# Hash-routed experts behind a gated recurrence: row numbers carried in the sorted rows, tiles read in twos, weights cast by the DMA of GpSimd, eleven sorted groups, 54 chunks scanned by way of TensorE

## The chip, the cores and the metric

The kernel runs on one core of one Trainium2 chip. The metric is the device time of one execution in microseconds, the median of three. A profile is one further execution, taken with the hardware profiler, with a trace of every instruction and of every DMA packet.

## What is computed

The reference has two parts. The first is a gated recurrence over the sequence; the second sends each of its output rows through one of eight small networks, chosen by a hash of the token's id.

```
x, f_logit: [4, 5056, 256] f32;  lower_bound: [256];  token_ids: [20224];  w1: [8, 256, 1024];  w2: [8, 1024, 256]
f = lower_bound + (1 - lower_bound) * sigmoid(f_logit)
for t in range(5056):
    h = f[:, t] * h + (1 - f[:, t]) * x[:, t]
    y[:, t] = h
expert = token_ids * 2654435761 % 8
out[rows of e] = relu(y[rows of e] @ w1[e]) @ w2[e]
```

The multiplier leaves 1 modulo 8, so the expert is the low three bits of the id. Each expert gets 16 of 128 tokens on average.

## The kernel before

The 20224 tokens are cut into 158 chunks of 128 (32 positions of the four sequences), and these into 24 blocks (`TS`), most of them of eight chunks.

**Scan.** A block's `f_logit` and `x` are loaded with one row per token, but the scan instruction runs along the free axis, so features have to lie on partitions. In the first `KS = 7` blocks (46 chunks) TensorE transposes each chunk (L743), ScalarE and VectorE make the gate (L747 to L758), VectorE scans (L773), TensorE transposes back (L812) and ScalarE or VectorE evicts to `yT` (L826). In the other blocks VectorE transposes in 32 x 32 pieces, before and after (L926, L988), with its scan in L969. A block begins where the one before it ended, so scans follow one another.

**Sort.** Each token's place in `srt`, a buffer in DRAM with 21 tiles of 128 rows (`CAP`) for each of eight experts, is worked out from the ids by one-hot tables, scans and matmuls (`rank_*`). Chunks before the middle fill an expert's rows from below and chunks after it from above, and some tiles in between are zero-filled first (`fill`). GpSimd scatters `yT` to `srt` row by row, one indirect DMA per chunk (L676). For seven blocks the last four chunks go another way: a one-hot matrix (L1010) sorts 512 rows by expert in TensorE (L1017), the result is put to a scratch buffer, and eight plain DMAs of 104 rows from SyncE (`move`, L1052), with addresses read from registers (`regs`), move each expert's segment to its place. Scatters after such a block wait for its moves.

**Row numbers.** The output rows have to go back to their tokens. For each block `tb` builds one-hot matrices of rank and tile on VectorE (L1093 to L1104), `tpe` multiplies them on TensorE (L1110) and `tadd` adds the result to a table and makes `row_i` (L1117 to L1126).

**Experts.** A tile of 128 rows of one expert is read when all blocks that can reach it have landed (`win`, `last`). A transposing DMA from SyncE brings it as `xe` (L1158). TensorE makes 1024 hidden values by 16 matmuls of 128 columns (L1168), ScalarE or VectorE applies the relu (L1177, L1179) to `hT`, TensorE goes down with eight matmuls of 256 columns (L1186), the result is evicted for two tiles at a time (L1194, L1196) and GpSimd scatters 128 rows to the output (L1200), one indirect DMA per tile.

**Weights** come through the same two staging buffers as `f_logit` and `x`, in f32, by SyncE (L640, L644), and ScalarE or VectorE casts them to bf16 (L653, L655).

**Order.** Each engine works through its instructions in the order in which they are written. The order of all tasks is a list found beforehand by a search over estimated costs and priorities, which is written into the file as a compressed string (`ORDER`) that also says whether ScalarE or VectorE takes each task that either can do. The costs and priorities in the `add` calls are remains of that search and change nothing at run time. Buffers are short rings (`xe` 8, `hT` 3, PSUM `hp` 2 and `op` 4), and a task that takes a buffer waits for the one that used it before.

After all this a flag is read; only where a count was outside its bounds does a slow loop over all chunks run. With these inputs it is not entered.

Of the kernel before, what the change touches and what calls it, by code (L numbers as in the profile page):

```python
# [11 lines left out]
FP32 = mybir.dt.float32  # L12
# [8 lines left out]
E = 8  # L21
# [6 lines left out]
KS = 7  # L28
# [7 lines left out]
RANGES = [(0, 6), (6, GA), (GA, MID), (MID, NG)]  # L36
FILL = (9, 12)
FB = {GA: [9, 10, 11], MID: [13, 15, 17, 19]}
FS = [k for a in (GA, MID) for k in FB[a]]
GF = len(FS)  # L40
FA = ()
SEG = 104
XF = 3
OFF, TABD = 20.0, 25.0
W0, W1 = -70.0, 6.0
# [3 lines left out]
    "c-"  # L49
    "jrsgQ8_Q5CFiayEC?J+qP}nww06Q&U<6qwr$(CZCkrPQ5D9d;jAx<&ib(ttUnvTMzMj6u^4PH10z^8Glq?1;cTc`#A2~HEQJ}w5;J9nu#_ePi^+x"  # L50
    "=W8$*WY#Iy93}($Z=Ga&hfh}d8#b%4yc(aKuV-rjyGo7Vl6U`D9ku_zLSSquE5u3$kvQ;br+rnm><!mL}%qFu_EWJr>uCc9b8=GS?noMS{*=|;w5"
    "ZlM*u{9<eTWjXC?B)#H&knGgY=_Bg*0C&XI9tzlnxyQ4-^C8GgX}bG!LphgEQdL4j+k5QEW6Imv7=@;Yi91S^X3?9#s0B{tT{W*E|`1lE-"
    "T9}s+KH1tH3V%OFjv^Xr{6&DyQN661(anoAPEao5F50!7nq(ulZ-}zPau{u@@{JTfl0vimVQ+Z626%?4e1-"
    "DzTSr4?DpUvRdpj+rXZ)jg0YEtS)<PzAzOeH(%LRc7@erCm96aSY_6cRbv=@HyPm(tIvLztWd>tVqMrzb3;95#Ph%}_Qo_~Rn1#d0IIW0po5$Kma"
    "oAg@OLa5bT$o4HOLIvAq(VyH0C#J&Dycj@Sb%w4Owx>3;Cd%dCCexW0s3GVQpD5^M_S}LZQDbKjaK`XKhSGe%t3ZY0U>#7)n3~Qxe*<NW2V`f{(0"
    "7sHb_t%0ds;i&cg@svJ~@@}VlB$o#I4!lUuJPy-V2KBg+f;4yh`lY~d-v4W^Pc2E=I1i2s=Zv*LgvY-"
    "~^=5d3>JZX@J=i_;U{6PjDk0%e(^AthKpg_<9;`3s>9yEkZycEyF>O;YxI4{F9^2|Y&pe)a88bN8Eisyzxyc|!>%LmnXVO|lc^BO#B&=`tAXXwQ%"
    "1pS}^WaCYsCa)OO;w5-?-"
    "V|2wdwvx!3N7KjU(b8<D6Ax}9khbB(2iH)jd(uO4l46HL3e1v6Y>On4S%3I@Gj6A@|$9;6Yt0?K;57RbcHm$Jw!E4c|YDPc<76pw7fBI9&~{AydL"
    "iy^x-{W0B;fG<lUe@AH)Yi4&Dpu^OiwX-imh#R&vdX@`1b#^oG8?YcPvDJ~(L2&+<9^3NOM#yc<tphXk{EcRn;2&OIN;!*~Nep0DHQ`6WJ&&*kTM"  # L60
    "e^|{g@U{Gr4-Y2r`N1&WkT-`(d?FtVm-&cbWUwG;!w10RpeJ7#wB?KVD87MD2|n?w-"
    "0+RTR=zhF0*m?7U{i3B@8|o19{els1XcKEzKo|62l+tQ#((l3d>S9kuLU>x7hW5N!XchfSiY2h<_Gu~m;hV&bZ+6X5BP0<Jt)MQ!FRqqxWTsvhl3"
    "r#FgP9*U}O32;ApTj*cFW7xA<><Cm0Te%?y4w*b@{qkAf%a33uQjtC-"
    "1;1yA`i9tKPJbT|?`^CyDm+`w4)#h>~IK{!l=aqu_@!E9IrGvHn@9!9`7-Vr9j{ouL(6Z{RL*nfNuFfkJXco8gv%p#h|BBI(e{7tYJxSb4h;Z-"
    "1PU&tYr!^>bJEP>a-NRW0G#I-HNTG#=5Ai7uznZ!KECSItM9PA2M32|&Z5nm{~4q{j>NTAIr4#O%q#rwc<h-DMl(|i-O6jLCkZ6y-"
    "f(Qpp3i&3y1BG{cUU95(Lb_28)5p6pW+dd2~!Dg5b?_n=Qvb!L$%_Sn+oAA<qh9i(t?1NMyw=H6xKt8br?!s1h<x`6^VmGXTBK8EN6>UUbQP}3ON"
    "1>P~D$c_UQQ79VCn1?Q1`DBzZ7-^dx50jBD^5Xi+d=$-0ye3rCSI!xa2aNai!c=m+LE?}eF3-"
    "N3Y4~GY&kIvl8EYdJ0uq$_y_+FYT5&E6+ZHNP{?)^x8V-du=k;?K-"
    "S4Vg?IcVl(+ABDVtu@vK4Ixu?^n%3U;=51|MJnG!>`8*#}U`b`^)9v;7EjM1A`T=82i2i?{|~pn>RS8;Os8u6Pb7#Y2dQ4Mk&t*xmN9pVV;SZ5&L"
    "FA<@(Rh9=?@y!C_ZIQtbCzEi#IL5P82cE0!nLqt9C4c`0LKzK?F6=&g#A8bE+j>BwXd;@=>kBEdC1;)fP5N;QU>oCIJfXMhAjIAx=Vmg!<3wzszw"  # L70
    "yx+aPK!Ds0zQTkEFO-uOGIE}<0Dusnu&h4xman>i71!^SBw5O6ArL%AwEXMq?iIz;svqDrpI@{rL}9sKr7`L@e?xRc##u#+TG#@EVU)gL@_~p^%-"
    "!Log|XsGP_481WbVEMJoKJE{W8b3-e+YTyEFe+*lrq;0jwAOJF{nEH>J8mgGed9XHvrVzbDI(Xbv0SroJ4dYd1|h&=eiZxP>pNgOS<+C-"
    "QZ6Jj<@gS+fDJ4Kuoqr_CP*KW5P>@=aImIbgF7Q}tF6xPCA@~1D3`)xj18Y^HKtb&(qQ*4RZF$WgLE_lEe!m?NnE8-"
    "4Y39r~v=C=K%UfZkUosA%`iK^HEYvTz4vJU?C^|1j~!|V2lxMOeFx1ugK#GCe*xGPGtd*Y~gV&B-u)?q|h9h+fu?2k{yecK8TiWYcW^v2fs-sX`V"
    "v8ZW-"
    "4{amtiq8bf5B9n3gl(~m>5RkhrR|1?#7BF}zOa4pfgOp5#djOoMRMJ70QSWm*ijmsf_ddw9Ebr%ku~v=ePwIlC!1Twa{aI|dh9F*VQlwTM3r%50o"
    "erGV=tVKA&lmtyBYXHByzt*JNzkPxKa3948}ixD~`svvL}wiotVn~5f;CR;W!l&yYZOXC6SBqs|dp(I1SUv&teQFbu)1l4#hMwo=fKb`Ytk^3&#a"
    "G0Sn3muCVMR*I`VTUw#p@a5~P$g&5yW#0-wfIhfEDlF8j79D)DTBwT_iToLzA%$Dh06<5YB#f7q%<e`-"
    "A0CtnBaT#WG%W(}Bm+P^d+<<ejs4L;h%bs#AR+HOMgid1%S6yz$l5QjJ!m6&TEbEToWSocRv6rmjcHl}}f!8pz+>M*Cf-"
    "B{+$vW;J=8zBZ5O$Xm_TXMTif6FCtmv}KvzS$~&@rs*>dDgX9L|+B-"  # L80
    "C?ZcYPl>jlYEK|TxE9)Yr6~B+YNS&+;wc|F5(STp)GhE8@ul~)a8_y(7W5%Lq5Vj?j~Nw)^eD<gD3DY4tGP`GyH%d*H_-"
    "f=Ll*uwv=yhp8SoHTFHKLAMVEpAyilKEndMk@*~cX?c_Urf)PV8slWSy_i%uFfdgGs`h<}nOh!_t@Fg~tgIrtr2Y=#dXWU{LS%o{I_qag*#n0GWe"
    "!(RYLQQ1g#!5vP8sn@RCx0QqKh&f{Cvm(3dVtX=a%hBGB$qnpMmk3Kae_mNKoebbdW{ijuZu(p=oQAIB-BiP!}hX+oG-"
    "s(YMSI?({d?@Q$pJ6F3C|Y8>Oc!@~TWkQ79Kh30;=kWm1YkaVRn^b35b;nTBS`sG+zN4bsv|myEW#=`t~`ay#7tx!Pr*eQt^@NEzw6%uZ`v8A?t?"
    "DILY9{c@e#AWymql!Fes!!9>XmNVr|xn8bud1#|cL76BgMGqZvg=mw@OSj~0S(u8^9k<z4r+id|;?Zt*Lr#^~<SzHdWv1fv#FeEZt|FD7a<s+Wca"
    "7+-t4-zUnbfKV?QzZMxqRxT$x3ua-jna-dwEKxqB_);9=M0DBt3F9sWQ!wDe0?=5h|=|QI)W_j?`)S!hLWZDP|}uHKwz&F4dzit_PJ;&8Z1BrH}5"
    "L%TEO;3$>%~t~4E!=Vc4(L`P+N>O-I0OIM%H$-"
    "xv={cxk`mn%g*sWWw;mJ|yjsxXS6`chSjq8__eVbT06*NY6r^e1F=Us4UB<FX&6^VO&e^`;nVDE)NF{cCqo26RFGcHz{JrczfLL9u*m>Q6;f2LIW"
    "`_HleNAI~?S0W^^;#R(0gHq?z`hvJ6f`#Drhb*GeSG$mAyMp6Qm!VjW9auTKYOnJ(v#?S)VM45alUsR2yxPCG%r_6pD&85{eol^TOehPI}xqLh*q"
    "h^p&GsA{ci008knxy8_xUdo`kuR;%_(e33_R<PkOe<*{CGlmwR8!O%66y?XrnR(+mQYo{g|^dQSzN87w7$IJYAYS23cinuAIj>xtHge?YU-"  # L90
    "2vYQCJ$t!nsv)J^ROtFC6#`ml;VkIJj|(=0kfCn%r)Coj`Zs^n|>+P<f%><`d&T1MH_1bRfx{bAZgC#i=zMfufPYUUG!>iR2mk8-"
    "FZRLh^E({wfLJl&xBzJ<!E`l>I~OI7jXsh;0J4SYY}&@ZKzw3}M`w{)M5(nczvdaDaGRTWg%Xb&~^H|a4wpkvg?5AX>?x2UzhO@-"
    "7Cnx$URacbqWtJgH!_xE*t6F*3`@y<unZ|EUCp^J2v!u(V6{v9bjP+g*VDqJm5gFVwBb%%!d1%9ULq&ljvlnCBaB%L_)fi|kRI-&ka-"
    ")N}cthT7(D!Vp*lj^K~(RW&?rm1I?B*gV^`WQCCi*V49bz6nuUDQ?;_@tp>e*6FJ{s~*`r>itNijJ=1{ZC1JJ<2D8xju!SuVREp)noill|Z*s9aM"
    "XjNXOJOR7#y#@A8?o^&@>+ojjCJr_wLzGmZAK!ava>Ki1FjN%TKTr?cp#{y7!WCG|m7R_pM;lvOYD6V-"
    "B`LyuE6bbg&$?^XMKHl1F_);m;AolEagg>_>cK^F*5stf82x|FV>i|9i>j^3t9>vDR6I^fs%eZIav>?7(Fq1<}6U+s(PBmSr#uUhGhy1Y)NSNbx#"
    "ovx~r>mj;=_PUrZu2=YKx~8tB8|byZq3)_z`O`j=uC9;!COVHk<6G;VdVnsWD~6x&jdX3j&NtPkd>ehtkJIh-"
    "N#9I&2;ZQ(>9%^3&a2P*IyxnE*Xva!-BI__J#=q9Q1{WDbn4J~HB^V|LHeAktn2CK;WPCxJy@rKkY1sOhqurpw9$3-T-{kO(c^WhP#4`dJZ-"
    "3@9;qkmKyTI)!o&2G@b!A49;MTTX6e~_s-CBp>S=m@cz@kbkJjm7nVzFp>IHg(UZ|~J74Gydy<Bh6tMzo9A+%Ai(PQ=2@ELlO-lrGq-"
    "FlneulMLhdW=30zE`i++x0<xD14pXsdwlj`mp{F4ZxtQ"  # L100
# [54 lines left out]
def kernel(  # L155
# [19 lines left out]
    WMAX = 8 * max(window(k)[1] - window(k)[0] + 1 for k in range(NB))  # L175
# [10 lines left out]
    srt = dram.tile([E * CAP, D], BF16, name="srt")  # L186
    scr = [dram.tile([4 * P + SEG, D], BF16, name=f"scr{i}") for i in range(3)]
    i32a = consts.tile([P, NT], I32, name="i32a")
    iota_lo = consts.tile([P, P], BF16, name="iota_lo")
    iota_hi = consts.tile([P, NT], BF16, name="iota_hi")  # L190
# [8 lines left out]
    Tab = consts.tile([P, 2, NT], FP32, name="Tab")  # L199
# [17 lines left out]
    ids7 = rp.tile([P, GA], I32, name="ids7")  # L217
    tok = rp.tile([P, NH, 32], I64, name="tok")
    tlow = rp.tile([P, NH * 32], I32, name="tlow")
# [13 lines left out]
    nmax = rp.tile([1, 2], FP32, name="nmax")  # L233
    handt = rp.tile([P, 8, 4], FP32, name="handt")
    row_id = rp.tile([P, NG], I32, name="row_id")
    row_t = rp.tile([P, NG], I32, name="row_t")
    lowt = rp.tile([P, NG], FP32, name="lowt")
    hight = rp.tile([P, NG], FP32, name="hight")
    eb_all = rp.tile([P, NG], BF16, name="eb_all")
    v1 = rp.tile([P, NG], BF16, name="v1")  # L240
    v2 = rp.tile([P, NG], BF16, name="v2")
    lo_h = rp.tile([P, NG], BF16, name="lo_h")
    hi_h = rp.tile([P, NG], BF16, name="hi_h")
# [12 lines left out]
    pl.pool("xe", 8)  # L256
    pl.pool("hT", 3)
    pl.pool("ob", 4)
    pl.pool("tb", 1)
# [6 lines left out]
    def init_pool():  # L266
        make_identity(nc, idf[:])
        nc.gpsimd.iota(i32a[:], pattern=[[1, NT]], base=0, channel_multiplier=0)
        make_upper_triangular(nc, up1[:], diag=False)

    def init_pool1():
# [5 lines left out]
        nc.gpsimd.memset(m8[:, :, 0:1], 0.0)  # L277

    def init_pool2():
        nc.gpsimd.memset(Tab[:], 0.0)  # L280
        nc.gpsimd.iota(
            oneh.rearrange("p c s -> p (c s)").bitcast(I32)[:, 512:1024].rearrange("p (j q) -> p j q", j=4),
            pattern=[[1, 4], [4, P]], base=0, channel_multiplier=0,
# [30 lines left out]
    def init_dve2():  # L314
        nc.vector.tensor_copy(iota8[:], i32a[:, :E])
        nc.vector.tensor_scalar(up1[:], up1[:], -1.0, None, op0=ALU.add)
        nc.vector.tensor_copy(idn[:], idf[:])
# [1012 lines left out]
```

## Time and profile before

| | us |
|---|---|
| time, median of three (lowest, highest) | 662.44 (650.76, 664.62) |
| the profiled execution | 499.46 |
| its span, first to last instruction | 497.7 |
| busy in it: TensorE, VectorE, ScalarE, GpSimd | 389.5, 391.3, 328.9, 320.9 |
| last matmul ends, last scatter starts | 485.3, 487.7 |
| mean granted TensorE clock | 0.906 of full speed |

The profiled execution is a quarter shorter than the timed ones; the profile doesn't show why. "Busy" counts an engine's instructions but not the issue of DMAs, which is what SyncE does (in the trace "SPq"). The share of the DMA engines is packets' time over that of 16 engines, and can pass 1.0 where packets overlap. "Idle before" and the waits name the last thing that an instruction waited for.

### The profile page before, as it was taken

To read this page: it belongs to the slowest core of one execution; us is meant where nothing else is said; L and a number is where in the kernel's file an instruction comes from. 1 tells how busy PE (TensorE), PEld (TensorE's weight loads), DVE (VectorE), ACT (ScalarE), POOL (GpSimd) and SP (SyncE) were. 2 spreads that over 40 slices of the span, in tenths; PEclk is the share of its full clock that TensorE was granted. 3 is DMA by queue.
4 is the path that set the end of the run, shared out by engine and by line. 5 is a ranking of instruction groups with operands and counts; after the bars stand their busy time and mean duration, and the time that the engine had idled before them with its cause. 6 is when DMAs were issued, how large, how long until landed. Compare 5 with 4: busy or idle time off the path is not lost.

```text
span 497.7 us, 12978 instructions
## 1 busy us (share of the span) xinstructions
PE 389.5 (78%) x4690; PEld 350.0 (70%) x4690; DVE 391.3 (79%) x916; ACT 328.9 (66%) x475; POOL 320.9 (64%) x385
## 2 busy tenths in 40 slices
PE   3655557885686997866997889799869978899990
PEld 2544446774586887756896779689859868899980
DVE  2799746899999899949898969898897896854430
ACT  2479445788787888656997769687757564565430
POOL 8066162457775767737777577776657776777772
PEclk9756588998798999979999899999989989999996
DMA  8999999999799989897999799699747773454521
GB/s 212 375 369 379 296 298 346 307 311 244 189 229 207 218 210 238 211 211 184 193 223 216 184 195 231 128 205 213 216 139 179 208 165 102 142 144 125 149 98 45
DMA packets 116035, 106.21 MB, mean 213 GB/s; under 512 B 59953, under 2 KB 99869, under 8 KB 115967
## 3 DMA queue, kind: packets, MB, share of 16 engines
q1 hardware_dynamic: 101743, 76.04, 60.5%
q0 software_dynamic: 12352, 29.28, 23.3%
q8 instruction: 38, 0.62, 0.6%
q10 hardware_dynamic: 1872, 0.02, 0.2%
q14 instruction: 30, 0.25, 0.2%
HBM read 61.47 MB, written 37.09 MB: 198 GB/s over the span
## 4 chain that ended last, share of the span: by engine, by line
PE 38%; DMA 17%; DVE 6%; ACT 5%; issue 4%; POOL 2%; SPq 2%; POOLq 0%; DVEq 0%; ACTq 0%
PE hp L1168 19%; PE op L1186 16%; DMA xe<-srt 14%; ACT hT L1177 3%; PE so L1017 2%; POOL out_dram L1200 2%; DVE y L969 2%; DMA f_t<-in_f_logit_dram 1%; SPq L1158 1%; DVE xT L952 1%; DVE sT L926 1%; DMA srt<-yT,pos_i 1%; ACT sT L940 1%; DMA x_t<-in_x_dram 1%; DVE xT L926 1%
## 5 line engine op out<-in xcount | busy, mean ns | idle before, releaser
L1200 POOL DMA_INDIRECT out_dram<-ob,row_i x168 | 172.8, 1028 | 75.9 <-issue 43.6
L1168 PE MATMUL hp<-xe,w 128*128 128x128 bf16 x2688 | 181.1, 226 | 50.7 <-DMA xe<-srt 40.4
L1177 ACT ACTIVATE hT<-hp 128x1024 bf16<-128x1024 f32 x152 | 153.7, 1023 | 85.7 <-PE hp L1168 67.4
L1168 PEld LDWEIGHTS <-w 128*128 128x128 bf16 x2688 | 167.8, 101 | 60.2 <-DMA xe<-srt 32.9
L676 POOL DMA_INDIRECT srt<-yT,pos_i x130 | 136.7, 1052 | 90.5 <-issue 33.8
L1186 PE MATMUL op<-w,hT 128*128 128x256 bf16 x1344 | 177.8, 284 | 9.4 <-ACT hT L1177 5.5
L1186 PEld LDWEIGHTS <-hT 128*128 128x128 bf16 x1344 | 131.4, 102 | 29.6 <-ACT hT L1177 7.7
L969 DVE TENSOR_TENSOR_SCAN y<-sT,y,xT 128x256 bf16<-128x256 f32 (+2 forms) x128 | 78.4, 645 | 0.2
L940 ACT ACTIVATE sT<-sT,lb_c,c_c 128x256 f32<-128x256 f32 (+2 forms) x109 | 57.9, 566 | 6.8 <-DVE sT L926 6.7
L1194 ACT COPY ob<-op 128x512 f32<-128x512 f32 x68 | 39.1, 585 | 17.7 <-PE op L1186 15.5
L926 DVE STREAM_TRANSPOSE xT<-x_t 128x512 f32<-128x512 f32 (+1 forms) x64 | 38.6, 619 | 13.7 <-DMA x_t<-in_x_dram 11.8
L952 DVE SCALAR_TENSOR_TENSOR xT<-sT,xT 128x512 f32<-128x512 f32 x56 | 37.2, 675 | 15.4 <-ACT sT L940 15.1
L1179 DVE TENSOR_SCALAR hT<-hp 128x1024 bf16<-128x1024 f32 x16 | 19.5, 1221 | 28.7 <-PE hp L1168 24.6
L926 DVE STREAM_TRANSPOSE sT<-f_t 128x512 f32<-128x512 f32 (+1 forms) x64 | 38.0, 613 | 0.1
L899 ACT ACTIVATE f_t<-f_t 128x1024 f32<-128x1024 f32 (+1 forms) x29 | 29.6, 1027 | 6.5 <-DMA f_t<-in_f_logit_dram 4.9
L773 DVE TENSOR_TENSOR_SCAN y<-sT,y,xT 128x256 bf16<-128x256 f32 (+1 forms) x48 | 31.4, 691 | 0.3
L1093 DVE TENSOR_TENSOR A<-iota_lo,lo_h 128x512 bf16<-128x512 bf16 (+1 forms) x41 | 26.8, 653 | 0.9 <-PE tp L1110 0.9
L812 PE MATMUL yp<-idn,y 128*128 128x128 bf16 x88 | 12.6, 266 | 17.3 <-DVE y L773 10.5
L743 PE MATMUL tf<-idf,f_t 128*128 128x128 f32 x92 | 17.7, 339 | 9.6 <-DMA f_t<-in_f_logit_dram 7.0
L988 DVE STREAM_TRANSPOSE yT<-y 128x256 f32<-128x256 f32 (+2 forms) x68 | 22.8, 363 | 0.0
L812 PEld LDWEIGHTS <-y 128*128 128x128 bf16 x88 | 7.6, 115 | 21.0 <-DVE y L773 15.8
L752 ACT ACTIVATE sT<-sT,lb_col,c_col 128x256 f32<-128x256 f32 x39 | 21.7, 596 | 0.2
(142 smaller groups left out, 314.2 us busy)
## 6 DMA issues: line engine op xcount, KB each, us to landing
f_t<-in_f_logit_dram SPq DMA_DIRECT2D x50, 256.0 KB
x_t<-in_x_dram SPq DMA_DIRECT2D x50, 256.0 KB
f_t<-in_moe_w_dram SPq DMA_DIRECT2D x8, 1024.0 KB
x_t<-in_moe_w_dram SPq DMA_DIRECT2D x8, 1024.0 KB
f_t<-in_f_logit_dram SPq DMA_DIRECT2D x10, 512.0 KB
x_t<-in_x_dram SPq DMA_DIRECT2D x10, 512.0 KB
srt<-scr SPq DMA_DIRECT2D x56, 52.0 KB
xe<-srt SPq DMA_TRANSPOSE x168
```

The costliest lines, as they stand in the source:

```text
L676: bi = nc.gpsimd.indirect_dma_start(out=srt[:], out_offset=bass.IndirectOffsetOnAxis(ap=pos_i[:, G0[k] + m:G0[k] + m + 1], axis=0), in_=T[ ...
L773: nc.vector.tensor_tensor_scan(yv[:, h, b, :tt], T["sT", un][:, h, c], T["vT", un][:, h, c], init, op0=ALU.mult, op1=ALU.subtract,)
L899: nc.scalar.activation(v, v, AF.Sigmoid)
L926: nc.vector.transpose(o, i_)
L940: nc.scalar.activation(v, v, AF.Identity, scale=c_c[:, c:c + 1], bias=lb_c[:, c:c + 1])
L952: nc.vector.scalar_tensor_tensor(x_.rearrange("p s c l -> p (s c l)"), f_.rearrange("p s c l -> p (s c l)"), 1.0, x_.rearrange("p s c l -> ...
L969: nc.vector.tensor_tensor_scan(yv(T["y", k])[:, cp, :L, s], T["sT", k, u][:, s, n, :], T["xT", k, u][:, s, n, :], init, op0=ALU.mult, op1= ...
L1168: nc.tensor.matmul(hp[:, f, :], lhsT=w1_sb[e][:, h, f * P:(f + 1) * P], rhs=xe[:, h, :], start=(h == 0), stop=(h == 1),)
L1177: nc.scalar.activation(hT[:], T["hp", j, e][:], AF.Relu)
L1186: nc.tensor.matmul(op[:, h, :], lhsT=T["hT", j, e][:, f, :], rhs=w2_sb[e][:, f, :], start=(f == 0), stop=(f == FF - 1),)
L1194: nc.scalar.copy(ob[:], T["op", n // 2][:])
L1200: bi = nc.gpsimd.indirect_dma_start(out=out, out_offset=bass.IndirectOffsetOnAxis(ap=row_i[:, c:c + 1], axis=0), in_=T["ob", n // 2][:, h, ...
```

## The change

It is one bundle of edits that hang together, with an order of its own (another `ORDER` string).

- **Row-number columns.** A row of `srt`, of the scratch buffers and of `yT` grows from 256 to 288 bf16 values (512 to 576 bytes). The added 32 columns repeat the token's row number as two values (`vv`), copied in once for each block (`id_cols`). When the tiles of column `j` are complete, SyncE reads four bytes of each of their 8 x 128 rows (`ids_in`), and two small VectorE operations make `row_i`. The table and its one-hot matrices go.
- **Tiles in twos.** For eight pairs of neighbouring tiles (`DUO`) both are read by one transposing DMA of 256 rows, and the up matmuls take 256 columns, four of the eight hidden slices at a time. Five tiles of each expert are still read singly, and these are paired across two experts for the eviction. `xe` has six buffers of twice the size, `hT` four.
- **GpSimd weight casts.** GpSimd loads each weight straight to bf16, with the cast in the DMA (`SW = range(8)`), instead of SyncE with casts on ScalarE and VectorE.
- **Eleven sorted groups** in place of seven: two before the middle, and all nine blocks of eight chunks after it. Three of them (`FA`) have their moves issued by ScalarE. Row numbers are sorted with the rows (`sort_ids`).
- **KS = 9:** two more blocks of 128 positions each sequence, eight chunks, are scanned by way of TensorE. Loads of these blocks from the fifth on are two per block, not four.
- The zero fill covers five tiles of each expert instead of three, and the flag also tests that the counts reach the filled region and that a segment isn't too short.

Its core:

```
-KS = 7
+KS = 9
-FB = {GA: [9, 10, 11], MID: [13, 15, 17, 19]}
+RA = 46
+FB = {RA: [9, 10], MID: list(range(12, 21))}
-FILL = (9, 12)
+FILL = [(8, 11), (11, 13)]
+RW = 288
-FA = ()
+FA = (2, 5, 8)
+DUO = [(1, 2), (3, 4), (5, 6), (7, 8), (12, 13), (14, 15), (16, 17), (18, 19)]
+XE, HT = 6, 4
+SW = range(8)
...
-    srt = dram.tile([E * CAP, D], BF16, name="srt")
+    srt = dram.tile([E * CAP, RW], BF16, name="srt")
...
+                    if v:
+                        nc.gpsimd.dma_start(w1_sb[e][:], moe_w1[e].rearrange("(s h k) f -> k s h f", s=2, h=2))
+                    else:
+                        nc.gpsimd.dma_start(w2_sb[e][:], moe_w2[e].rearrange("(q p) d -> p q d", p=P))
...
+    def id_cols(eng, k):
+        o = T["yT", k][:, :NGS[k], D:].rearrange("p m (r s) -> p m r s", s=2)
+        i_ = vv[:, G0[k]:G0[k] + NGS[k], None, :].to_broadcast((P, NGS[k], (RW - D) // 2, 2))
...
-        def tb(c0, c1, k=k, jlo=jlo, W=W):
-            nc.vector.tensor_tensor(
-                A[:, c0:c1, :], iota_lo[:, None, :].to_broadcast((P, n, P)),
-                lo_h[:, gs, None].to_broadcast((P, n, P)), op=ALU.is_equal,
-            )
...
-        def tpe(k=k, W=W, ng=ng):
-        def tadd(k=k, jlo=jlo, W=W):
+        def ids_in(j=j):
+            bi = nc.sync.dma_start(
+                row_v[:, j, :, :], srt.rearrange("(e c) d -> c e d", e=E)[j * P:(j + 1) * P, :, D:D + 2]
+            )
+        def ids_row(j=j):
+            nc.vector.scalar_tensor_tensor(
+                pi[:], row_v[:, j, :, 1], 256.0, row_v[:, j, :, 0], op0=ALU.mult, op1=ALU.add
+            )
+            nc.vector.tensor_scalar(row_i[:, E * j:E * j + E], pi[:], -1.0, None, op0=ALU.add)
...
-            bi = nc.sync.dma_start_transpose(xe[:], srt[r0:r0 + P, :])
+            bi = nc.sync.dma_start_transpose(xe[:, :, :w], srt[r0:r0 + w, :D])
...
-            for f in range(FF):
+            for n, f in enumerate(fs):
                 for h in range(2):
                     nc.tensor.matmul(
-                        hp[:, f, :], lhsT=w1_sb[e][:, h, f * P:(f + 1) * P], rhs=xe[:, h, :],
+                        hp[:, n * w:(n + 1) * w], lhsT=w1_sb[e][:, h, f * P:(f + 1) * P], rhs=rhs()[:, h, :],
```

## The prediction

> **What bounds the kernel now.** I read the engine table and the slices first, then stages, then waits, then the queue of SyncE.
>
> ```profile
> span 497.7 us, 12978 instructions
> ...
> PE 389.5 (78%) x4690; PEld 350.0 (70%) x4690; DVE 391.3 (79%) x916; ACT 328.9 (66%) x475; POOL 320.9 (64%) x385
> ...
> DMA  8999999999799989897999799699747773454521
> ```
>
> No engine is full, but three are near 80% or idle only at the ends. DMA is at nine tenths or more for most of the first two thirds. Three stages separate what an average mixes:
>
> ```profile
> core 0: us, PE busy (x) PEld busy (x) DVE busy (x) ACT busy (x) POOL busy (x), PEclk, DMA share, GB/s
> 25.00:125.00 100.00, 65.91 (x675) 56.50 (x675) 82.59 (x191) 69.88 (x106) 51.59 (x49) 0.77 1.06 318
> 125.00:375.00 250.00, 208.62 (x2591) 188.75 (x2592) 222.26 (x505) 189.72 (x275) 173.03 (x166) 0.94 0.92 202
> 375.00:488.00 113.00, 102.93 (x1357) 94.72 (x1354) 73.69 (x175) 60.28 (x80) 84.18 (x84) 0.98 0.55 145
> ```
>
> Columns: stage, its length, busy time and (instructions) of each engine, granted clock, DMA share. TensorE idles 34 us in the first stage (DMA over 1.0, low clock), 41 us in the second (VectorE at 89%), 10 us in the third. With 13 us of the first 25 and 10 us after 488 this is all of its 108 us idle (497.7 - 389.5). In the third stage GpSimd is full although it reads 74%: its indirect DMAs follow each other every 1.28 us, 0.97 busy and 0.30 of issue.
>
> ```profile
> 392.28 0.97 POOL L1200 DMA_INDIRECT out_dram<-ob,row_i  x1 [0.31 <-issue]
> 393.55 1.01 POOL L1200 DMA_INDIRECT out_dram<-ob,row_i  x1 [0.30 <-issue]
> 394.88 0.97 POOL L1200 DMA_INDIRECT out_dram<-ob,row_i  x1 [0.31 <-issue]
> ```
>
> The engine that no busy row shows is SyncE, whose queue issues in order. In the middle of the kernel:
>
> ```profile
> 320.93 2.46 SPq L1158 DMA_TRANSPOSE xe<-srt  x2
> 323.43 1.08 SPq L876 DMA_DIRECT2D f_t<-in_f_logit_dram  x2
> 324.62 1.17 SPq L1158 DMA_TRANSPOSE xe<-srt  x1
> ```
>
> There is no gap: a transposing tile read holds the queue for 1.2 us (168 records sum to 222 us, with some long ones), a load 0.5. All SyncE issues and register loads sum to some 390 us. The waits agree on what TensorE lacks:
>
> ```profile
> PE hp L1168 <- DMA xe<-srt: 40.4, 21, 4.7
> PEld L1168 <- DMA xe<-srt: 32.9, 19, 3.2
> ```
>
> (Total us, times, longest. The matmul and its weight load see the same tile late; they aren't added). So: TensorE is the longest work, it starves for tiles, and tiles are late because VectorE makes rows slowly and SyncE hands tiles out slowly; the end is shared by TensorE and GpSimd.
>
> **What the Trainium skill says.** "DMA: Bandwidth & Descriptors", section "Issuing engines are not separate DMA queues", says that issuing from several engines saves sequencer time alone; here that is just what is short, so moving weights to GpSimd and three groups to ScalarE helps SyncE and doesn't add bandwidth. Its section "SWDGE vs HWDGE vs iDMA" leaves a cast during the transfer to GpSimd, which is what the change uses; the trace has no such transfer. Its section "How a descriptor splits into AXI transactions" counts 18 beats for 576 B on a 256 B boundary and 25 off it; 512 B would be 16 by the same rule. No run shows this yet. "TensorE: Matmul & The Clock Gate", section "Back-to-back issue gap", gives some 81 ns for a sustained 128-column matmul with its weight load, but the trace runs 32 of them in 1.79 us, 56 ns. The trace decides: there is no weight-load penalty to be won back.
>
> **The change, part by part.** Busy time unless said.
>
> Row numbers. The table of row numbers goes: on VectorE L1093 26.8, L1097 10.7, L1101 11.2, L1104 11.2, L1117 4.6, L1123 3.3, L1126 4.3, together 72 us, and four splits of ranks, 4 us; on TensorE 158 matmuls of L1110, 8.8 us. In exchange each block gets a copy of its number into 32 columns (23 or so of about 0.3 us, some on ScalarE: 8 us), each sorted group 16 tiny matmuls and a 0.2 us copy (11 x 0.45 TensorE, 11 x 0.2), and 21 reads of 1024 four-byte pieces with two 0.17 us VectorE operations each (7 us). The 16-byte packets of the ids took 9 ns each in the packet records, so a read costs 1024/16 x 9 ns = 0.6 us of the 16 DMA engines, up to 1 us in a crowd: 12 to 20 us in all.
>
> Rows of 576 B. Bytes of sorting traffic grow by an eighth; by beats an unaligned row could cost 25/16. All packets of the software queue took 110 us of 16 engines, a quarter of that is row scatters; 4 to 15 us more. Groups, padding and the larger zero fill add some 5 MB to 106 MB.
>
> Tiles in twos. 64 pairs (8 x 8) and 40 single tiles make 104 reads in place of 168. The cost of issuing 256 rows isn't in the trace: at least the 1.2 us of one tile, at most two, 2.4. I take 1.4, since issue is one instruction: 104 x 1.4 = 146 against 222 us, 76 less; at the other end it is nothing saved. TensorE gets 1024 fewer matmuls, but 16 of 256 columns take 1.75 us (L1186's x16) against 1.79 for 32 of 128: 64 x 0.04 = 3 us. A pair must be complete before it is read, so its first tile starts later; buffers for six pairs replace eight tiles. Matmuls of the next unit wait behind it in TensorE's order.
>
> Weights. 32 casts go (L653 18.3 us of ScalarE, L655 9.8 of VectorE), 16 loads leave SyncE (9.5 us) and become 16 GpSimd DMAs of about 0.9 us (L367, L346 show 0.75 to 0.9), in the first 100 us, where GpSimd is half idle: nothing on the path. They are spread at 14 us an expert, so late experts can't start early.
>
> Sorted groups. Four more: TensorE 4 x 14.35/7 = 8.2 us, VectorE 4 x 1.2, and 16 fewer row scatters. All nine groups after the middle are sorted, so 20 fewer there (four more before): 20 x 1.28 = 26 us off the queue that ends the kernel. SyncE keeps eight groups, 64 moves of 0.58 us against 56; three groups hold ScalarE about 8 us each, with its evictions queued behind them and TensorE waiting for those.
>
> 54 chunks. Eight chunks move to TensorE at (32.75 + 13.18)/46 = 1.0 us each, 8.2 us; VectorE loses their transposes, (76.6 + 22.8)/112 x 8 = 7 us. Fewer, larger loads: 18 issues, 9.5 us of SyncE.
>
> Sum: TensorE 389.5 - 8.8 + 5 - 3 + 8.2 + 8.2 = 399 us. VectorE 391 - 76 - 10 - 7 + 22 = 320. SyncE 390 - 76 - 9.5 - 9.5 + 5 + 12 = 312. GpSimd about as before, but 26 us less late. So the starved engine gets 10 us more and its suppliers 70 to 78 us less. Of its 108 idle us I expect the first 25 and the tail to stay (23), the first stage to go from 34 to 26 because DMA still fills it, the second from 41 to 16 because both suppliers drop from nine tenths to about 70%, the third from 10 to 6. That is 71: 399 + 71 = 470 us, 0.944 of the profile.
>
> The timed runs are 662.4 us, 1.33 times the profile, and no view says why. I carry the ratio over: 662.44 x 0.944 = 626.
>
> **The rivals.** *TensorE or DMA is the bound in the timed runs.* Their longer time would come of a slower matmul clock or slower memory; then relief of the others is worth nothing and the added 10 us of matmuls (2.5%) or 20 to 35 us of DMA on 427 (5 to 8%, part of it hidden) is paid: 662 x 1.025 = 679, slower. For: DMA share 0.92 to 1.06 over 350 us, clock 0.77 in the first stage. Against: TensorE idles 108 us here.
>
> *The suppliers' relief is hidden.* Pairs that complete later, weights spread out and an issue of 2.4 us per pair leave TensorE as starved as now; only the 26 us of GpSimd count, and TensorE's own end catches them after 4: 10 us of work against some 14 us of idle time won, 497.7 - 4, or 657.
>
> *Instruction count matters.* If the timed runs pay per matmul, 4690 falls to about 3800 (-1024 - 158 + 48 + 64 + 176), 19%; half of that is 598.
>
> **How the numbers follow.** Forecast 0.52 (626); counts 0.12 (598); hidden 0.15 (657); bound 0.21 (679). Faster by over 2% (under 649): 0.64; within: 0.15; slower: 0.21. The range runs from the counting case, 595, to almost the bound case, 676; about one in ten lies on each side.
>
> **What would show it.** L1093 to L1126 gone; tile reads 104 on SyncE at about 1.4 us; TensorE about 399 us busy, VectorE about 320; in the second stage TensorE idle under 25 us and its wait for tile reads below 25 us; in the last 100 us GpSimd with gaps over 0.30. Wrong, if a paired read holds SyncE over 2 us, if waits for weights appear in the first 100 us, if DMA stays at 0.9 or above to 375 us with tiles still late, or if evictions wait behind the moves that ScalarE issues.

## The result and the profile after

| | before | after | ratio (95%) |
|---|---|---|---|
| time, median of four (lowest, highest) | 657.78 (650.76, 664.62) | 603.58 (602.35, 609.72) | 0.9255 (0.9161 to 0.9349) |

The changed kernel is 54 us faster, and the time lies in the predicted range, 22 us under the prediction. From the profile of the changed kernel, taken in one of these timed executions (PE is TensorE's matmuls, PEld its weight loads, DVE VectorE, ACT ScalarE, POOL GpSimd):

```profile
span 600.6 us, 11000 instructions
...
PE 435.9 (73%) x3798; PEld 356.5 (59%) x3798; DVE 376.9 (63%) x804; ACT 270.9 (45%) x392; POOL 312.1 (52%) x386
...
DMA  8899999999997991399783457686285435434331
...
PE 36%; issue 22%; DMA 11%; DVE 10%; POOL 7%; another core or an unknown queue 6%; ACT 5%; SPq 2%; ACTq 1%; POOLq 0%; DVEq 0%
...
L1203 PE MATMUL hp<-xe,w 128*128 128x256 bf16 (+1 forms) x1664 | 197.5, 269 | 81.6 <-issue 43.2
```

The span is 100 us longer than that of the profile shown of before, yet no engine is fuller: TensorE is busy for 73%, and DMA falls to two or three tenths in slices of the second half. On the chain that ended last (the last instruction, followed back through what released each step) 22% is "issue", time in which the engine waited for nothing that the profile shows. The waits of the same trace (total us, times, longest):

```profile
POOL out_dram L1234 <- ACT ob L1228: 118.3, 29, 13.2
PEld L1203 <- issue: 91.1, 78, 7.0
ACT hT L1212 <- remote: 89.6, 16, 11.2
...
PE hp L1203 <- issue: 43.2, 48, 5.1
```

and how such a stretch looks on TensorE (start, length, instruction; in brackets the idle time ahead of it):

```profile
225.16 0.10 PEld L1203 LDWEIGHTS <-w 128*128 128x128 bf16 x1 [0.61 <-issue]
225.87 0.31 PEld L1203 LDWEIGHTS <-w 128*128 128x128 bf16 x2 [0.61 <-issue]
226.25 0.36 PEld L1220 LDWEIGHTS <-hT 128*128 128x128 bf16 x2
227.30 0.56 PEld L1220 LDWEIGHTS <-hT 128*128 128x128 bf16 x4 [0.69 <-issue]
228.72 0.13 PEld L1220 LDWEIGHTS <-hT 128*128 128x128 bf16 x2 [0.86 <-issue]
```

One to four weight loads, then some 0.6 to 0.9 us without one, and no wait for data that the trace shows. ("remote" is a releaser that the trace doesn't name.) This is not the picture on which the prediction was built: the trace of before has only `PEld L1168 <- issue` at 24.7 us in 19 waits. The row of weight loads can pause while matmuls run, so I call a *stall* only a stretch of over 0.3 us in which TensorE runs neither, and ahead of whose end no semaphore was waited for. Worked out from the records, the trace of before has none, and this one 78, together 45.3 us. So the first question was whether the edit makes these stalls, or whether a timed execution is another thing than the 498 us profile. It is the second. In three of the four groups of runs below the kernel before took 501 to 503 us beside each experiment, and in the last 658 us, on a chip on which it had taken 501 us some minutes earlier. I call the kinds the 500 us level and the 650 us level. The first three groups and the 498 us profile are at the first, the timed runs above and the last group at the second. Within a group all times were of one kind, so each experiment is set against the kernel before in its own group, and experiments of different groups are compared by these ratios.

### The profile page after: what moved, and what is told of

The parts are those of the page before. It is cut to its first block, busy times and chain, and to the rows that moved or that the text cites. A ratio compares the mean times of both kernels' runs of the same rounds, so it can differ in the third digit from the quotient of the medians.

```text
span 600.6 us, 11000 instructions
## 1 busy us (share of the span) xinstructions
PE 435.9 (73%) x3798; PEld 356.5 (59%) x3798; DVE 376.9 (63%) x804; ACT 270.9 (45%) x392; POOL 312.1 (52%) x386
## 4 chain that ended last, share of the span: by engine, by line
PE 36%; issue 22%; DMA 11%; DVE 10%; POOL 7%; another core or an unknown queue 6%; ACT 5%; SPq 2%; ACTq 1%; POOLq 0%; DVEq 0%
PE hp L1203 16%; PE op L1220 14%; POOL out_dram L1234 5%; DMA xe<-srt 4%; DMA x_t<-in_x_dram 4%; DVE y L902 3%; PE so L733 3%; ACT hT L1212 2%; DMA srt<-yT,pos_i 2%; POOL srt L709 2%; DVE xT L887 1%; PE tf L872 1%; ACT ob L1228 1%; PE tx L872 1%
## 5 line engine op out<-in xcount | busy, mean ns | idle before, releaser
L1203 PE MATMUL hp<-xe,w 128*128 128x256 bf16 (+1 forms) x1664 | 197.5, 269 | 81.6 <-issue 43.2
L1212 ACT ACTIVATE hT<-hp 128x1024 bf16<-128x1024 f32 x137 | 138.3, 1026 | 209.1 <-remote 89.6
L1203 PEld LDWEIGHTS <-w 128*128 128x128 bf16 x1664 | 148.6, 104 | 115.7 <-issue 91.1
L1220 PEld LDWEIGHTS <-hT 128*128 128x128 bf16 x1344 | 136.5, 104 | 51.3 <-issue 24.7
L709 POOL DMA_INDIRECT srt<-yT,pos_i x114 | 115.9, 1016 | 80.7 <-ACT yT L702 31.0
L1214 DVE TENSOR_SCALAR hT<-hp 128x1024 bf16<-128x1024 f32 x31 | 37.8, 1220 | 81.8 <-PE hp L1203 47.2
L1062 DVE STREAM_TRANSPOSE sT<-f_t 128x512 f32<-128x512 f32 (+1 forms) x56 | 35.6, 649 | 11.9 <-ACT yT L702 6.3
L1062 DVE STREAM_TRANSPOSE xT<-x_t 128x512 f32<-128x512 f32 (+1 forms) x56 | 35.6, 647 | 3.5 <-DMA x_t<-in_x_dram 3.4
L1230 DVE COPY ob<-op 128x512 f32<-128x512 f32 x21 | 14.3, 682 | 27.2 <-PE op L1220 13.6
L733 PE MATMUL so<-yT,oneh 128*128 128x256 bf16 x176 | 26.1, 292 | 6.3 <-issue 5.2
L876 ACT ACTIVATE sT<-tf 128x512 f32<-128x512 f32 x27 | 16.1, 596 | 31.7 <-PE tf L872 15.3
L1076 ACT ACTIVATE sT<-sT,lb_c,c_c 128x256 f32<-128x256 f32 (+2 forms) x51 | 29.4, 590 | 1.4 <-DVE sT L1062 1.0
L872 PEld LDWEIGHTS tf<-idf,f_t 128*128 128x128 f32 x108 | 18.7, 201 | 14.6 <-issue 6.7
```

The source lines that it names most:

```text
L709: bi = nc.gpsimd.indirect_dma_start(out=srt[:], out_offset=bass.IndirectOffsetOnAxis(ap=pos_i[:, G0[k] + m:G0[k] + m + 1], axis=0), in_=T[ ...
L733: nc.tensor.matmul(t[:, j, :], lhsT=oneh[:, c, (2 * v + j) * P:(2 * v + j + 1) * P], rhs=T["yT", k][:, 4 + c, :D], start=c == 0, stop=c == 3,)
L872: nc.tensor.transpose(view(t[:, h, :]), T[which, k][:, u * nch + n, h * P:(h + 1) * P], idf[:])
L1062: nc.vector.transpose(o, i_)
L1203: nc.tensor.matmul(hp[:, n * w:(n + 1) * w], lhsT=w1_sb[e][:, h, f * P:(f + 1) * P], rhs=rhs()[:, h, :], start=(h == 0), stop=(h == 1),)
L1212: nc.scalar.activation(hT[:], T["hp", key][:], AF.Relu)
```

## The experiments

**The kernel before, and the changed kernel, at the 500 us level.** Before, unchanged:

> The kernel before, unchanged, to see its trace in an execution of the length that was timed (650 to 665 us), not the 498 us of the first profile. Supply theory (TensorE starves for tiles because VectorE and SyncE are slow): the extra 150 us are waits of TensorE for tile reads, well above the 40 us of the first profile, and busy times are as there. Issue theory (TensorE stalls before single instructions that wait for nothing, as in the trace after): gaps of about 0.7 us before single matmuls or weight loads, none in the first profile, sum to 70 us or more on TensorE, and waits for tile reads stay near 40 us or below.

Measured 502.3 us with a trace like the first one (TensorE 391.1, VectorE 392.3 busy); other runs of the kernel before in the same group had a median of 501.35. So there is no trace of a long execution of before. The changed kernel, unchanged, in the next group:

> The changed kernel itself, beside the kernel before. In the first comparison before took 658 us and this one 604; in the runs since, before took 501 us and its trace shows no stall of 0.7 us before instructions that wait for nothing. Supply theory: the relief of VectorE and SyncE counts in any execution, ratio 0.92 to 0.95 here too. Issue theory: what was won were stalls of instruction streams that are absent in executions of 500 us, so the ratio is 0.99 to 1.01 where before takes 500 us, and about 0.925 where it takes 650.

Measured 498.60 us against 502.78 beside it, ratio 0.9894 (0.9844 to 0.9945). Its page, its stages (start and end, length, busy time and instructions of TensorE, its weight loads, VectorE, ScalarE and GpSimd, granted clock, DMA share, GB/s) and its waits:

```profile
span 499.3 us, 11000 instructions
...
PE 397.1 (80%) x3798; PEld 345.3 (69%) x3798; DVE 376.9 (75%) x804; ACT 271.1 (54%) x392; POOL 311.9 (62%) x386
```

```profile
25.00:125.00 100.00, 61.89 (x529) 53.08 (x527) 91.59 (x216) 46.16 (x82) 61.57 (x108) 0.72 1.11 253
125.00:375.00 250.00, 211.99 (x2117) 184.21 (x2116) 198.31 (x390) 163.49 (x227) 155.45 (x153) 0.95 0.98 215
375.00:488.00 113.00, 108.93 (x1076) 97.06 (x1075) 72.71 (x155) 50.80 (x68) 81.47 (x82) 1.00 0.66 156
```

```profile
PE hp L1203 <- DMA xe<-srt: 23.0, 17, 3.5
ACT f_t L1035 <- DMA f_t<-in_f_logit_dram: 21.6, 6, 8.8
DVE pi L1161 <- DMA row_v<-srt: 21.1, 7, 8.7
...
PEld L1203 <- issue: 17.2, 13, 4.3
...
ACT yT L955 <- DMA w<-in_moe_w_dram: 11.2, 1, 11.2
...
POOL srt L709 <- DMA w<-in_moe_w_dram: 9.2, 4, 5.1
...
PE hp L1203 <- DMA w<-in_moe_w_dram: 6.3, 1, 6.3
```

The same instructions take 101 us less of span here than in the timed execution. There TensorE is busy for 39 us longer (435.9 against 397.1, at a granted clock of 0.852 against 0.910) and idle for 62 us longer (164.7 against 102.2). Stalls are 45.3 us of that idle time and 0 of it here, so they are shown, but directly they are less than half of the difference. How much of the rest follows from them, and how much from the lower clock, is not shown. Other waits shrink meanwhile: the one for tile reads goes from 23.0 to 3.9 us. No stalls appear here, as in the profile that was predicted from, so the prediction's parts are tested at this level. And here the whole bundle is worth 1.1%, not 5.6%.

**Reads in twos.** Each pair is read by two transposing DMAs of 128 rows; the matmuls stay at 256 columns.

```
-            bi = nc.sync.dma_start_transpose(xe[:, :, :w], srt[r0:r0 + w, :D])
+            for c in range(0, w, P):
+                bi = nc.sync.dma_start_transpose(xe[:, :, c:c + P], srt[r0 + c:r0 + c + P, :D])
```

> The changed kernel with each 256-row tile read issued as two of 128 rows, so 168 transposing reads as before (64 more, some 77 us more of SyncE's queue), matmuls of 256 columns kept. Supply theory: tiles come late again and much of the gain is lost, 620 to 645 us. Issue theory: SyncE has room, 600 to 610 us.

Measured 539.62 us, 1.0661 (1.0555 to 1.0767) of before. Against 0.9894 for the bundle, the 64 further reads cost 7.7% of 502 us, 39 us or 0.6 us a read. The trace with paired reads and then the one with two reads each (nanoseconds, least/median/most of one issue on SyncE):

```profile
L1193 SPq DMA_TRANSPOSE xe<-srt x104: 1167/1237/3677, 62.7 to 477.5; - x104
```

```profile
L1196 SPq DMA_TRANSPOSE xe<-srt x168: 1167/1242/4073, 62.5 to 519.4; - x168
```

and TensorE's wait for tiles with two reads each:

```profile
PE hp L1204 <- DMA xe<-srt: 35.4, 19, 4.3
```

With pairs, 64 of the 104 reads are of 256 rows, so the median speaks for them: a read of 256 rows holds the queue no longer than one of 128, and a pair saves about one whole issue. Summed, the reads hold SyncE for 233 us instead of 160, and about half of these 73 us reaches the end. What SyncE issues comes later all round (in a trace of the longest of the four runs, 543 us): TensorE's wait for tiles rises from 23.0 to 35.4 us, VectorE's for row numbers from 21.1 to 30.7 and for loads of `x` from 9.7 to 21.5. DMA itself is no rival here, since the hardware queue's packets take no more time (50.6% of 541.3 us against 55.3% of 499.3).

**Matmuls of 256 columns.** The up matmuls of a pair are cut in two, with one read for the pair.

```
-                for h in range(2):
-                    nc.tensor.matmul(hp[:, n * w:(n + 1) * w], ..., rhs=rhs()[:, h, :], ...)
+                for c in range(0, w, P):
+                    for h in range(2):
+                        nc.tensor.matmul(hp[:, n * w + c:n * w + c + P], ..., rhs=rhs()[:, h, c:c + P], ...)
```

> The changed kernel with the 256-column up matmuls of the pairs cut into two of 128 columns each, so 1024 more matmuls and 1024 more weight loads on TensorE (3798 to 4822), the same reads, order and arithmetic. Supply theory: TensorE's work grows by 3 us at full clock, so 603 to 608 us. Issue theory: time goes with the number of TensorE instructions, so most of what the change won comes back, 630 to 650 us.

Measured 505.16 us, 1.0082 (1.0053 to 1.0112). So 1024 fewer matmuls are worth 1.9%, 9 us, three times what I gave them, although TensorE's busy time is the same (397.2 against 397.1). Where the 9 us arise was not measured apart.

**Both undone.** The two edits above together:

```
-            bi = nc.sync.dma_start_transpose(xe[:, :, :w], srt[r0:r0 + w, :D])
+            for c in range(0, w, P):
+                bi = nc.sync.dma_start_transpose(xe[:, :, c:c + P], srt[r0 + c:r0 + c + P, :D])
...
+                        nc.tensor.matmul(hp[:, n * w + c:n * w + c + P], ..., rhs=rhs()[:, h, c:c + P], ...)
```

> The changed kernel with its pairs undone in both ways: two reads of 128 rows and up matmuls of 128 columns. Supply theory: SyncE's 77 us come back and tiles are late, 1.06 to 1.08 of before, as the run with two reads alone (1.066). Issue theory: as the supply theory where before takes 500 us; where it takes 650, the 1024 matmuls come on top, 1.0 or more.

Measured 547.07 us, 1.0885 (1.0844 to 1.0925). Without the pairs the rest of the bundle is 9% slower than before. It runs in an order that was searched with pairs in it, so this is what pairs are worth here, 10% (547.07 - 498.60 = 48 us), and not what a bundle without pairs could reach with an order of its own.

**The table away, in the kernel before.** `tb`, `tpe` and `tadd` return at once, and `row_i` is filled with a constant list. The way of the output rows back to their tokens is left out; the scatters themselves stay.

```
-        nc.gpsimd.memset(Tab[:], 0.0)
+        nc.gpsimd.iota(row_i[:], pattern=[[P, NT]], base=0, channel_multiplier=1)
...
         def tb(c0, c1, k=k, jlo=jlo, W=W):
+            return
```

> The kernel before without the making of the row-number table (no one-hot matrices, no 158 table matmuls, no additions); rows go to the output by a constant list of all rows in place of their own, so what is left out is the inverse permutation. VectorE loses 72 us. Supply theory: VectorE's relief is a main part of the gain, ratio to before 0.95 to 0.97. Issue theory: 158 of 4690 matmuls less, ratio 0.98 to 1.0.

Measured 499.98 us, 0.9962 (0.9933 to 0.9991). From its page and its waits:

```profile
PE 385.0 (77%) x4532; PEld 345.9 (69%) x4532; DVE 331.4 (67%) x690; ACT 328.6 (66%) x475; POOL 318.0 (64%) x385
```

```profile
PE hp L1171 <- DMA xe<-srt: 51.7, 26, 4.8
```

Sixty microseconds of VectorE go and the time falls by two. TensorE's wait for tile reads even grows, from 40.4 to 51.7 us, which fits rows that come sooner and tiles that SyncE hands out no faster, though this run doesn't show it apart. VectorE at 89% in the middle stage was company of the bound, not the bound.

**The new row-number reads away, in the changed kernel.** `ids_in` and `ids_row` return at once, with the same constant list, so here too the way back to the tokens is left out.

```
         def ids_in(j=j):
+            return
...
         def ids_row(j=j):
+            return
```

> The changed kernel without the 21 reads of four-byte row numbers and their VectorE operations; rows go to the output by a constant list of all rows, so what is left out is the row numbers' way back. If output scatters wait for these reads (20.6 us of VectorE waiting for them in the trace of the run with 128-column up matmuls), it is 2 to 4% faster than the changed kernel; if the reads are hidden, the same within 1%.

Measured 488.02 us, 0.9724 (0.9684 to 0.9764). The reads cost 1.7% of before, about 9 us; TensorE's busy time in the middle 250 us rises from 211.99 to 217.95 without them. The hardware queue of the loads and reads takes 53.1% of 484.9 us instead of 55.3% of 499.3, 19 us less of the 16 DMA engines (with the reads, then without):

```profile
q1 hardware_dynamic: 113183, 62.11, 55.3%
```

```profile
q1 hardware_dynamic: 91343, 62.02, 53.1%
```

The constant list writes the output rows one after another, but that is not what saves: the packets of the output scatters take no less time with it (239 ns on average against 232). In its kernel this form of the row numbers costs more than the table with its 60 us of VectorE did in the other (1.7% against 0.4%).

**Their reads later.** The four-byte reads and their two VectorE operations move to just ahead of the first scatter that uses them, since `pi` makes VectorE wait 21.1 us for the data.

```
+    order.sort(key=lambda t: at_[id(t)] if not t.name.startswith("ta") else max(at_[id(t)], pos[...] - 3.5))
```

> The changed kernel with the two VectorE operations that turn a read of row numbers into output addresses moved later in the order, to just ahead of the first output scatter that needs them (for most columns some ten VectorE operations later). If the 1.7% that the reads cost is VectorE standing at the head of its queue before a read has landed (21 us in 7 waits), half of it or more comes back: 0.975 to 0.983 of before. If it is the reads' own load on DMA and SyncE, or the scatters' wait for the numbers, no change or slower: 0.988 to 1.0.

Measured 506.32 us, 1.0111 (1.0027 to 1.0194): worse than where they stood. The cost of the reads is not only where VectorE waits for them; which part of the 9 us is the DMA time, which the waits, and which SyncE's issue of 21 more DMAs (0.57 us each at the median, 11 us in all), stays open.

**Weights by GpSimd, in the kernel before.**

```
-            T["stg", e, v] = ld.tile([P, NGM, D], FP32, name="xf"[v] + "_t", tag="xf"[v])
...
+            if v == 1:
+                nc.gpsimd.dma_start(w1_sb[e][:], moe_w1[e].rearrange("(s h k) f -> k s h f", s=2, h=2))
+            else:
+                nc.gpsimd.dma_start(w2_sb[e][:], moe_w2[e].rearrange("(q p) d -> p q d", p=P))
+            return
```

> The kernel before with its weights loaded and cast by the DMA of GpSimd at the places in the order where SyncE loaded them; no casts on ScalarE (18 us) and VectorE (10 us), 16 issues fewer on SyncE. Supply theory: a small gain in the first 100 us, ratio 0.98 to 0.99. Issue theory: 0.99 to 1.01. GpSimd might wait at a weight's place in its queue: then slower, 1.01 to 1.03.

Measured 505.52 us, 1.0103 (1.0014 to 1.0192): about 1% dearer, in an order that was not searched for it. Two views answer (waits, then the two DMA queues, with those of before at this level last):

```profile
PE op L1190 <- DMA w<-in_moe_w_dram: 9.6, 2, 8.1
POOL srt L680 <- DMA w<-in_moe_w_dram: 5.5, 4, 1.8
```

```profile
q1 hardware_dynamic: 91247, 59.26, 52.1%
q0 software_dynamic: 22848, 37.67, 33.6%
```

```profile
q1 hardware_dynamic: 101743, 76.04, 60.0%
q0 software_dynamic: 12352, 29.28, 22.6%
```

Waits for weights appear on TensorE and even ahead of GpSimd's scatters. The software queue takes 33.6% of 499.0 us against 22.6% of 500.5 before, 55 us more of the engines, and the hardware queue 40 us less (52.1% against 60.0%): weights that are cast during the transfer cost about 15 us of DMA more than before.

**Loads from ScalarE's queue.** To see whether SyncE's issue is the limit, the loads of the VectorE blocks go to ScalarE, first in the changed kernel, then in the kernel before.

```
-LA = ()
+LA = range(NB)
```

> The changed kernel with the 120 loads of the blocks scanned on VectorE issued from ScalarE's queue at the same places in the order, not from SyncE's; some 64 us less for SyncE, as much more for ScalarE, which is busy 271 of 499 us. Supply theory (SyncE's queue, with waits at its head, is what holds the changed kernel at 499 us): 0.95 to 0.975 of before. If SyncE no longer matters: 0.985 to 1.0. If loads behind ScalarE's own waits come late: over 1.0.

```
-                    lambda t=t, b=b, f=load: f(t, b, nc.sync),
+                    lambda t=t, b=b, f=load: f(t, b, nc.scalar),
```

> The kernel before with the 136 loads of its VectorE blocks issued from ScalarE's queue, some 72 us off SyncE. Supply theory (SyncE issues without gaps and TensorE waits 40 us for tiles): 0.95 to 0.98 of before. If the issue of tile reads isn't what makes tiles late: 0.99 to 1.01. ScalarE is busier here (329 us), so loads may come late: then over 1.01.

Measured 526.06 us, 1.0505 (1.0400 to 1.0610), and 538.85 us, 1.0751 (1.0667 to 1.0835). The gain of the supply theory did not come in either: in the changed kernel loads on ScalarE come late (`DVE xT L1062 <- DMA x_t<-in_x_dram: 27.1, 6, 15.3`, against 9.7, 4, 3.4 before the edit), and TensorE waits longer for ScalarE's relu (34.3 us against 14.5). On SyncE they are a hint only: TensorE's wait for tile reads falls, from 23.0 to 2.6 us in the changed kernel and from 40.4 to 9.1 in the kernel before, as it would if SyncE's queue makes tiles late; but a kernel that is held up elsewhere also asks for its tiles later. What they do say is that ScalarE, which waits and computes in the same order, is a poor place for these loads.

**The three groups' moves back on SyncE**, at the 650 us level:

```
-FA = (2, 5, 8)
+FA = ()
```

> The changed kernel with the three sorted groups that ScalarE moves given back to SyncE at the same places in the order: 24 moves, three puts and three register loads, some 20 us more for SyncE and none of ScalarE's 13 us of waits for the moves' data. If ScalarE as an issuer holds its evictions up more than it relieves SyncE: 0.975 to 0.985 of before, better than the changed kernel. If SyncE is what is short: 1.0 to 1.03. If before takes 650 us here, the chip stalls as in the first comparison; then this one is at 0.92 to 0.96 and its trace has stalls of 0.7 us on TensorE and SyncE.

Measured 604.44 us against 658.14 beside it, 0.9171 (0.9072 to 0.9269). This overlaps 0.9255 (0.9161 to 0.9349), so no difference from the bundle is shown either way. Its trace has the same stalls:

```profile
ACT hT L1212 <- remote: 109.8, 22, 9.4
PEld L1203 <- issue: 72.4, 53, 6.0
```

Both traces at this level thus show stalls as defined above, 78 of 45.3 us and 65 of 35.8 us; none of the twelve at the 500 us level has one. None of the kernels that compute everything is shown to be faster than the changed one.

## Why the prediction was right, and where it was not

The direction held at both levels, at 500 us by 1.1% only, less than the 2% that I called faster; the range held for the time that it was made for. That 603.6 lies as near to 626 as it does is partly luck: the size was put together from two errors that happened to point opposite ways.

**The step that failed was the last: "The timed runs are 662.4 us, 1.33 times the profile, and no view says why. I carry the ratio over".** The ratio isn't the same at the two levels: 0.9894 at 500 us, 0.9255 at 650 us. The extra time of a long execution is 657.78 - 501.35 = 156 us for the kernel before and 603.58 - 498.60 = 105 us for the changed one. That drop, 51 us, makes up nearly all of the 54 us that the bundle gains. What the extra time is in the changed kernel is shown in part: 45 us are stalls of TensorE, 39 us more busy time at a lower clock. Why it is less after the change is only argued. The lower clock alone doesn't give it: before falls from some 0.90 to 0.825 and the changed kernel from 0.92 to 0.845 (means of the runs), which at their busy times of 391 and 397 us is an estimated 36 and 35 us. That leaves stalls and what follows from them, and that before has more of them is not shown. They may go with the number of TensorE instructions (4690 to 3798 matmuls), which is what the rival "instruction count matters" supposed; at 598 us (599 by its own sum) it came nearest to the measured 603.6, with a chance of 0.12. They may as well go with SyncE's instructions, which stall too. A long trace of before and a long run with 128-column matmuls would tell the two apart, and neither exists. What causes the stalls is open too.

**Inside the profile I predicted 470 us and 498.6 came, so the sum for the 500 us level was 29 us too good.** The step that failed here is the idle time of TensorE, 102 us for the 71 of the sum. Term by term:

- *Reads in twos.* Shown, with 39 us of time, as the largest single gain. The issue of a pair is 1.24 us at the median, not 1.4, but some reads of either kind take longer: the 104 sum to 160 us, not 146. TensorE's wait for tiles fell from 40.4 to 23.0 us, under the 25 that I named as the sign.
- *TensorE's work, 399 us.* Measured 397.1. The 256 columns were put at 3 us, from matmuls and weight loads that follow without a gap, and are worth 9.
- *SyncE, 312 us.* All records of its queue sum to 355 us (396 before), so little more than half of the 78 us of relief came.
- *"The second from 41 to 16".* It was 38 (250 - 212), the first stage 38 instead of 26, and only the third, at 4, was a little better than the 6 that I took. Relief of VectorE was half of the reason for 16, and the table's removal measured 0.4%. Of the sign that I had named as contrary, DMA at 0.9 or above up to 375 us with tiles still late, the first half came: its share of the middle stage rose from 0.92 to 0.98. In the first stage the experts start later: the first down matmul is at 98.9 us, before at 60.7. Which edit does this was not tried; with the weights alone moved it is at 63.3.
- *The DMA bill.* The DMA engines' busy time rose from 418 to 453 us (the queues' shares, 83.6% of 500.5 and 90.8% of 499.3). Without the row-number reads it is 19 us less, the upper end of my 12 to 20, but I let them lie beside other work, and they cost 9 us of time. The weights are about 15; I had "nothing on the path" for them, and put alone into the kernel before they cost 1%. Waits for weights in the first 100 us, which I had named as a sign of being wrong, came too: in the changed kernel GpSimd's scatters wait for them three times between 80 and 90 us, 5.1 us at most, and TensorE for 6.3 us at 116. The Trainium skill ("DMA: Bandwidth & Descriptors", "Issuing engines are not separate DMA queues") gives to more issuing engines the sequencer's time alone, and no time came of it for the weights. The same page's count of beats ("How a descriptor splits into AXI transactions") I used too widely: its 25 is for a row that starts 224 bytes past a 256 B boundary. As a price the 25/16 is not borne out: ahead of the first output scatter a packet of eight rows took 191 ns at the median with 576 bytes and 162 to 172 with 512, 11 to 18% more, about as the bytes (12.5%), and fewer row scatters (114 against 130) make up for that.
- *VectorE, 320 us.* Measured 376.9. The edits left room, and the order of the change filled it. A scan step and a relu that either engine can do went over from ScalarE, as the groups of before and then of after at the 500 us level show (count, busy us, mean ns, idle before):

```profile
L1179 DVE TENSOR_SCALAR hT<-hp 128x1024 bf16<-128x1024 f32 x16 | 19.5, 1221 | 28.7 <-PE hp L1168 24.6 <-PE op L1186 4.1
...
L944 DVE TENSOR_SCALAR sT<-sT,c_c,lb_c 128x256 f32<-128x256 f32 (+2 forms) x27 | 9.2, 358 | 0.0
```

```profile
L1214 DVE TENSOR_SCALAR hT<-hp 128x1024 bf16<-128x1024 f32 x31 | 37.6, 1217 | 30.5 <-PE hp L1203 23.8 <-PE op L1220 6.7
...
L1080 DVE TENSOR_SCALAR sT<-sT,c_c,lb_c 128x256 f32<-128x256 f32 (+2 forms) x69 | 26.1, 397 | 0.2
```

  These two rows are 35 of the 57 us. I had counted the edits and left out the `ORDER` string, which decides the rest. ScalarE fell from 328.9 to 271.1 us, in part in exchange and in part because its weight casts (18 us) went.
- *Sorted groups and chunks.* Not tried apart: each hangs on the order. The gaps of GpSimd that I expected in the last 100 us didn't come: between 388 and 488 us it is busy for 72.4 us, before for 74.1, with output scatters that begin at 120 us instead of 72. Their share in the 499 us is open.

**The rivals.** "TensorE or DMA is the bound" was right that DMA was nearly full in the middle, and wrong for the timed runs, in which DMA has slices at two tenths. The slower matmul clock that it supposed is there (0.852 against 0.910), but what it carries is an estimated 35 us, and the change was faster all the same. "The suppliers' relief is hidden" described the 500 us level almost exactly (0.9894 against the 0.992 that it gave), but for another reason than it named: the pairs did pay, about 48 us, and the rest of the bundle took some 43 of them back. The row-number reads are 9 of these and the weights about 5, as far as a run of each alone tells, less 2 for the table. That leaves about 30 us that no run assigns to an edit; the order, which was searched with pairs in it, may be a large part.

## What to carry to other kernels

Before a ratio is carried from a profile to a timed run, see that the profiled execution has the timed length; where it hasn't, what the difference consists of is the first thing to ask. The transposing reads here cost SyncE's queue 1.24 us each, whether of 128 or 256 rows, so where TensorE waits for tiles and no busy row is full, fewer and larger reads are a gain to look for. Relief of a busy engine is worth what the waits say, not what its busy row says: 60 us off VectorE gave 2. A transfer called hidden needs DMA engines with room in that very stage.

## What was not expected of the hardware

- The same program takes 499 us in some runs and 604 us in others, and the kernel before 502 and 658; on one chip both lengths of before came, minutes apart. In the long executions TensorE stops between instructions with no wait that the trace shows. In the changed kernel 97 instructions start more than 0.4 us after the one before them without having waited for a semaphore, together 72 us, mostly in bursts of 5 to 10 us; in its 499 us execution none does. SyncE has 15 gaps over 0.4 us of this kind, against one in the 499 us execution; VectorE and ScalarE have none.
- Within a burst the instructions after stalls start 0.70 to 0.77 us apart, or twice that, in most cases. The two long traces have the same TensorE instructions, and 23 of the 65 stalls of one lie within ten records of a stall of the other, where about five would by chance. So the stalls come at about the same points of the program in both; whether the place or the time since the start decides can't be told, since the two traces run nearly in step. Slower transfers of instructions are not seen: the 31 packets of the queue `q8 instruction` took 1.06 us at the median in the long execution and 1.07 in the short one.
- Issue of a transposing read from SyncE takes 1.24 us at the median for 256 rows as for 128.
- A four-byte packet costs the DMA engines 9 ns at the median. The 21 reads of 1024 such packets each are 14 us of the 16 engines in their own packets (22.9 us of four-byte packets on this queue with them, 9.0 without), 19 us of the whole queue and 9 us of the kernel.
